# An attention-and-MoE kernel on one core: input queues, the ordering of v in wide products, w2 in 384 columns, and the last weight piece

## The chip, the core and the metric

The kernel runs on one core of one Trainium2 chip. A core has four engines that compute: TensorE (PE in the profile), VectorE (DVE), ScalarE (ACT) and GpSimd (POOL). SyncE (SP) only issues transfers. Products of PE land in PSUM, eight banks of 2 KB in each of 128 partitions; DVE and ACT read them from there into SBUF. Transfers between the chip's memory and SBUF are issued by SP, ACT or POOL, and 16 DMA engines carry them.

The metric is the device time of one execution in microseconds (us), as the median of several runs. Engine times from the profile are microseconds from the start of the span; single durations are in us unless marked ns.

## What is computed

Two layers follow each other. The first is a linear attention with a decaying state, for 4 batches, 8 heads, 768 positions, 48 channels per head:

```
cur  = (u * k_t) outer v_t
y_t  = r_t @ (state + cur)
state = w * state + k_t outer v_t
```

Its output, as x of 3072 rows and 384 columns, goes through a mixture of 8 experts with 4 slots each:

```
logits = x @ phi                       # 3072 x 32
d = softmax over the rows of logits    # which rows a slot takes
c = softmax over the slots             # which slots a row takes back
slot_out[e] = relu((d.T @ x)[e] @ w1[e]) @ w2[e]
out = c @ slot_out
```

w1 and w2 of all experts are 25 MB in float32, r, k and v 14 MB, the output 4.7 MB.

## The kernel before

**Attention.** A pair is two heads of one batch: 4 batches with 4 pairs each, so 16 pairs, numbered m. A pair's 768 positions are halved, and a step i works on one half: pair mu = i // 2, half i % 2. There are 32 steps, with five more ahead of them (i from -5) to fill the pipeline. A half is three blocks of 128 positions. In the code, the blocks are c, the halves g.

Everything is put in program order by hand: the function O keeps each instruction where it was written on its engine, so each engine executes its instructions in the order of the text, and only the waits between engines are added. In step i the order is:

1. a_pe(i+1) and mask_f(i+1): k times r for the next half into the two banks Ab, and DVE's masked copy AT.
2. y_pe(i) and y_evac(i): the result y of this half into columns 0 to 287 of the bank Yb, and ACT's copy of it into x (L372). One bank holds 512 float32 columns.
3. v_pe and v_evac, below.
4. m_pe(i+1) and z_evac(i+1): state and bonus terms into Mb, DVE's products Z (L341) and dv (L342).
5. prod (DVE, even steps), b_pe and kn (odd steps), and scale: POOL multiplies k or r by powers of w (L228) for a later pair.
6. route: what the mixture needs of finished rows: logits and transposes of x into Xb, ACT's copies xT, Le and LexpT; every fourth step also the slot sums (disp, L422 and L426) into columns 768 and up of T0 or T1.
7. t_pe and t_evac: six transposes of kr into T0 (even steps, k) or T1 (odd steps, r), and ACT's copy kT or rT (L241).

**v.** The inputs are loaded with six neighbouring positions of a sequence in one partition (three for v)[...]. v_cast turns a pair's v into bfloat16 (v_bf, L270; the first on POOL), and v_pe puts its rows in order: a product with a shifted selection matrix Q3 for each block c and each j of three, L284. Before the change it does so for one half at a time, two halves ahead: nine products of 96 columns into Vb, and one eviction of 288 columns by ACT (vn, L290).

**Loads.** SP issues w as a single row (L105) and then k, r and v in pieces of two heads. ACT preloads its table and issues w and u once more in another shape (L107, L108). The row w is spread over all partitions by a product (L177), and its logarithm and powers (W, L188 and L192) are needed before the first k can be scaled. POOL issues the weights (L135 for w1, L138 for w2) from step 13 on, in the middle of its scale work, once the last batch's k has landed (guard, L571). w2 takes the buffers of inputs that are used up (raw). The last expert's w2 comes in three pieces of 4, 2 and 2 of its 8 rows y (L576).

**The end.** The first layer of the experts is L623. The second layer (second, L656 to L662) runs four experts side by side in strips of 32 columns of PE; for each row y it takes w2's 384 columns in two products of 192, into Xb and into Yb. DVE and ACT scale a half each into so (L671, L672), and the output is a product of so with LexpT (L684), scaled by DVE and ACT (L686, L688) and written in nine pieces (L704).

Of the kernel before, what the change touches and what calls it, by code (L numbers as in the profile page):

```python
# [9 lines left out]
def kernel(  # L10
# [13 lines left out]
    B, H, S, D = r.shape  # L24
    C = 128
    nC = S // C
    Nn, Dm = out.shape
    ES = moe_phi.shape[1]
    E = moe_w1.shape[0]
    F = moe_w1.shape[2]  # L30
    Spe = ES // E
    nM = Dm // C
    nF = F // C
    nQ = H // 2
    G = 2
    L = nC // G
    T = L * C
    P2 = 2 * D
    nN = Nn // C
    nG = B * G  # L40
    nU = B * nQ
    nH = nU * G
    J = S // C
    JV = T // C

    f32 = mybir.dt.float32
    bf = mybir.dt.bfloat16
    i32 = mybir.dt.int32
    AF = mybir.ActivationFunctionType
    ALU = mybir.AluOpType  # L50

    def O(ins):
        return tc.keep_in_program_order(ins)

    pe, dve, act, pool, sp = nc.tensor, nc.vector, nc.scalar, nc.gpsimd, nc.sync

    big = ctx.enter_context(tc.tile_pool(name="big", bufs=1))
    cst = ctx.enter_context(tc.tile_pool(name="cst", bufs=1))
    wk = ctx.enter_context(tc.tile_pool(name="wk", bufs=3))
# [5 lines left out]
    EG = E // 2  # L65
# [4 lines left out]
    def w2_of(e):  # L70
        g, j = divmod(e, EG)
        return raw[1 + g][:].bitcast(bf)[:, j * eW2:(j + 1) * eW2].rearrange("p (y d) -> p y d", y=nF)

    def raw_of(which, b):
        return raw[b % NR][:, which * RW:(which + 1) * RW]
# [5 lines left out]
    Yb = psb.tile([128, 512], f32, name="Yb")  # L81
    Xb = psb.tile([128, 512], f32, name="Xb")
    Vb = psb.tile([128, 512], f32, name="Vb")
# [11 lines left out]
    w_row = early[0:1, 0:H * D]  # L95
# [5 lines left out]
    phi_f = late[:, 128:128 + nM * ES]  # L101
    wu = cst.tile([8, 128], f32, name="wu")
    wu3 = wu[:].rearrange("q (e s) -> q e s", s=64)
    O(dve.memset(wu[:], 1.0))
    O(sp.dma_start(out=w_row, in_=w.rearrange("(o h) d -> o (h d)", o=1)))  # L105
    O(act.preload_act_table_set("natural_log_exp_and_others"))
    O(act.dma_start(out=wu3[0:4, :, 0:D], in_=w.rearrange("(q e) d -> q e d", e=2)))  # L107
    O(act.dma_start(out=wu3[4:8, :, 0:D], in_=u.rearrange("(q e) d -> q e d", e=2)))  # L108
# [44 lines left out]
    Q3 = cst.tile([128, QW], bf, name="Q3")  # L153
# [59 lines left out]
    ones = cst.tile([128, 128], bf, name="ones")  # L213
    Le_t = [cst.tile([128, L, 128], bf, name=f"Le{j}") for j in range(2)]
    phi_s = cst.tile([128, nM, ES], bf, name="phi_s")
    phi_b = cst.tile([128, nM * ES], bf, name="phi_b")
    assert JV == nM
    acc = cst.tile([128, NA], f32, name="acc")
    guard = cst.tile([128, 1], f32, name="guard")
    st = {}  # L220

# [40 lines left out]
    def v_cast(m):  # L262
        b, q = divmod(m, nQ)
        vb = wk.tile([128, 2, G, JV, D], bf, name="v_bf", bufs=2)
        st["vb", m] = vb
        out, src = vb[:].rearrange("p h g j d -> p (h g j d)"), raw_of(2, b)[:, 2 * q * G * JV * D:2 * (q + 1) * G * JV * D]
        if m == 0:
            O(pool.tensor_copy(out, src))
        else:
            O(act.copy(out, src))  # L270


    def at(i):
        m, g = divmod(i, G)
        b, q = divmod(m, nQ)
        return m, b, q, g, b * G + g

    def v_pe(i):
        m, b, q, g, n = at(i)
        vb = st["vb", m]  # L280
        for c in range(L):
            for j in range(JV):
                o = C * c - j + JV - 1
                O(pe.matmul(Vb[:, c * P2:(c + 1) * P2], Q3[:, o:o + C], vb[:, :, g, j, :],  # L284
                            start=(j == 0), stop=(j == JV - 1)))

    def v_evac(i):
        vn = wk.tile([128, L, 2, D], bf, name="vn", bufs=3)
        st["v", i] = vn
        O(act.copy(vn[:].rearrange("p c e d -> p (c e d)"), Vb[:, 0:L * P2]))  # L290

    def a_pe(i):
        m, b, q, g, n = at(i)
        kT, rT = st["kT", m], st["rT", m]
        for c in range(L):
            t = slice((g * L + c) * C, (g * L + c + 1) * C)
            for e in range(2):
                s = slice(64 * e, 64 * e + 64)
                O(pe.matmul(Ab[:, e, c * C:(c + 1) * C], kT[s, t], rT[s, t]))  # L299
# [129 lines left out]
    def disp_ev(n, ds_p):  # L429
        if n == 0:  # L430
            O(dve.tensor_copy(acc[:], ds_p))
        else:
            O(dve.tensor_add(acc[:], acc[:], ds_p))
# [37 lines left out]
    Wf = [t[:].rearrange("p q j d -> p (q j d)") for t in W]  # L471
# [22 lines left out]
    for i in range(-5, nH):  # L494
        mu, odd = divmod(i, 2)
        if 0 <= i + 1 < nH:
            a_pe(i + 1)
            mask_f(i + 1)
        if pend:
            disp_ev(*pend.pop())  # L500
        if i == nH - 1:
            turn(n0, (2,), Vb[:].bitcast(bf), act)
            disp(n0 - 1, ds_t)
            le_t(n0 - 1)
            let_ev(n0 - 1, None, dve)
        if 0 <= i < nH:
            y_pe(i)
            y_evac(i)
        if 0 <= i + 2 < nH:
            v_pe(i + 2)  # L510
            v_evac(i + 2)
        if 0 <= i + 1 < nH:
            m_pe(i + 1)
            z_evac(i + 1)
        if odd == 0 and 0 <= mu + 1 < nU:
            prod_f(mu + 1)
        if odd and i > 0 and mu + 2 < nU:
            b_pe(mu + 2)
            b_evac(mu + 2)
        if odd and 0 <= mu + 3 < nU:  # L520
            scale(mu + 3, 0)
        if not odd and 0 <= mu + 2 < nU:
            scale(mu + 2, 1)
        route(i, 0)
        if 0 <= mu + 2 < nU:
            t_pe(mu + 2, odd)
            route(i, 1)
            t_evac(mu + 2, odd)
            if odd and i < 0:
                b_pe(mu + 2)  # L530
                b_evac(mu + 2)
        else:
            route(i, 1)
        if odd == 0 and 0 <= mu + 2 < nU:
            v_cast(mu + 2)
        route(i, 2)
        if i == nH - 3:
            turn(n0, (0, 1), T0, act)
        if i == nH - 2:
            turn(n1, (0, 1), T1, act)  # L540
        for f, j, q in T_AT.get(i, ()):
            f(j, q)
        if i in (-4, -3):
            wu_steps(i + 4)
        if i in Z_AT:
            q = Z_AT[i]
            O(act.activation(out=zt[:, q, 2, :], in_=zt[:, q, 0, :], func=AF.Copy, scale=wT[:, q:q + 1]))
        if i == 2:
            O(pool.memset(ones[:], 1.0))
            for t in Le_t:  # L550
                O(pool.memset(t[:], 0.0))
        if i == 3:
            load_kr(0, k, B - 1, 0, H)
            load_kr(1, r, B - 1, 0, H)
            for h0 in range(0, H, 2):
                load_v(B - 1, h0, h0 + 2)
        if i == 5:
            O(act.copy(phi_b[:], phi_f))
        if i == 6:
            for mi in range(nM):  # L560
                for j in range(nM):
                    o = C * mi - j + nM - 1
                    O(pe.matmul(Xb[:, mi * ES:(mi + 1) * ES].rearrange("p (j g s) -> p j g s", g=2, s=Spe),
                                Q3[:, o:o + C],
                                phi_b[:, j * ES:(j + 1) * ES].rearrange("p (g j s) -> p j g s", g=2, s=Spe),
                                start=(j == 0), stop=(j == nM - 1)))
            O(act.copy(phi_s[:].rearrange("p m s -> p (m s)"), Xb[:, 0:nM * ES]))
        if i == 28:
            O(pool.memset(uns, 0.0))
        if i == min(W_AT):  # L570
            O(pool.tensor_copy(guard[:], raw_of(0, B - 1)[:, 0:1]))  # L571
        for _ in range(W_AT.get(i, 0)):
            load_w(nw)
            nw += 1
    assert nw == 2 * E - 1
    for y0, y1 in ((0, 4), (4, 6), (6, 8)):  # L576
        load_w(nw, y0, y1)


# [29 lines left out]
    csr = cst.tile([128, 1], f32, name="csr")  # L609
# [8 lines left out]
    hT = [Wf[1].bitcast(bf)[:, g * F:(g + 1) * F].rearrange("p (y c) -> p y c", c=C) for g in range(2)]  # L618
    for g in range(2):
        for a in range(2):  # L620
            for mi in range(nM):
                for j in range(EG):
                    O(pe.matmul(hb[g][a][32 * j:32 * j + 32, 0:FH], uns[:, mi, g, j, :],  # L623
                                w1_all[:, g * EG + j, mi, a * FH:(a + 1) * FH],
                                start=(mi == 0), stop=(mi == nM - 1), skip_group_check=True))
            src = hb[g][a][:, 0:FH].rearrange("p (q y) -> p y q", y=nF)
            dst = h_sb[g][:, :, a * PH:(a + 1) * PH]
# [12 lines left out]
    def row_recip(a, z):  # L640
        O(dve.reciprocal(rsr[:, a:z], Mb[:, a:z]))

    HD = Dm // 2
# [7 lines left out]
        if g == 0:  # L651
            row_sums(0, 8)
    row_recip(0, 8)
    SO = [Xb[:, 0:HD], Yb[:, 0:HD]]

    def second(g, experts):  # L656
        for y in range(nF):
            for x in range(2):
                for j in experts:
                    O(pe.matmul(SO[x][32 * j:32 * j + 32, :], hT[g][:, y, 32 * j:32 * j + 32],  # L660
                                w2_of(g * EG + j)[:, y, x * HD:(x + 1) * HD],
                                start=(g == 0 and y == 0), stop=(g == 1 and y == nF - 1), skip_group_check=True))  # L662

    second(0, range(EG))
    second(1, range(EG - 2))
# [1 line left out]
    second(1, (EG - 2,))  # L667
    second(1, (EG - 1,))
    row_sums(8, 12)
    so = cst.tile([128, Dm], bf, name="so")  # L670
    O(dve.tensor_scalar_mul(so[:, 0:HD], SO[0], csr[:, 0:1]))  # L671
    O(act.activation(out=so[:, HD:Dm], in_=SO[1], func=AF.Copy, scale=csr[:, 0:1]))  # L672
    row_recip(8, 12)

    out_v = out.rearrange("(p n) m -> p n m", n=nN)
# [14 lines left out]
    i = 0  # L690
# [44 lines left out]
```

The softmax here doesn't subtract the row's maximum and nothing guards it: scores larger than these inputs give would overflow.

## Time and profile before

The median of three runs is 122.65 us (122.47 to 122.68).

| | us |
|---|---|
| profiled execution | 122.36 |
| its span | 120.5 |
| PE busy | 102.6 |
| DVE busy | 96.4 |
| ACT busy | 83.7 |
| POOL busy | 59.7 |
| first input issue of SP (w), then k | 0.74, 1.14 |
| first weight issue of POOL | 40.22 |
| first product of the second layer | 96.36 |
| last weight seen by PE | 103.83 |
| first output issue | 105.56 |

The span is what lies between the first and the last recorded instruction. The rest of the execution, 1.86 us, lies around it. A line of the timeline gives the start, the duration, the engine, the line of the kernel, the operation, output and inputs, the shape, and how many neighbouring instructions are merged; in square brackets stands how long the engine was idle before it and what released it. "PEld" is the loading of weights into PE, "SPq" and "ACTq" the issuing of transfers. The DMA row of the page has a digit for each fortieth of the span, about 3 us: the busy share of the 16 DMA engines in tenths. In the list of waits each line has the waiting engine and line, what it waited for, the sum in us and the number of times. L numbers are lines of the kernel before.

### The profile page before, as it was taken

How to read it: one execution, taken by the hardware profiler on the slowest of the kernel's cores; microseconds unless marked ns; L12 is line 12 of the kernel's file. 1: busy time of each engine (PE TensorE's matmuls, PEld its weight loads, DVE VectorE, ACT ScalarE, POOL GpSimd, SP SyncE). 2: the span in 40 equal slices, each digit the busy share in tenths (PEclk: the TensorE clock that was granted, in tenths of full speed). 3: DMA queues.
4: the chain of work that ended last, by engine and by line, in shares of the span. 5: the costliest groups of instructions: out<-in, count | busy, mean ns of one | idle time of the engine just before them, and what ended most of it. 6: DMA issues, size and time to landing. Idle time of an engine off the chain costs nothing.

```text
span 120.5 us, 4334 instructions
## 1 busy us (share of the span) xinstructions
PE 102.6 (85%) x1795; PEld 82.9 (69%) x1797; DVE 96.4 (80%) x187; ACT 83.7 (69%) x183; POOL 59.7 (50%) x70
## 2 busy tenths in 40 slices
PE   5996977799999999999999999999979996796000
PEld 1465866687887988898888898888866686583000
DVE  6899999999999999899999899999943510399000
ACT  4459769797978998888898988997963510299000
POOL 7349534599999999797677593101000000012000
PEclk9999999999999999999999999999999999999755
DMA  2999999999999999999999999999999998069992
GB/s 38 322 362 373 374 367 371 364 391 362 330 380 382 323 204 216 218 213 212 220 206 222 211 220 209 215 215 215 224 208 220 208 206 165 16 261 389 396 420 100
DMA packets 20925, 31.79 MB, mean 264 GB/s; under 512 B 1129, under 2 KB 18026, under 8 KB 20906
## 3 DMA queue, kind: packets, MB, share of 16 engines
q0 software_dynamic: 2960, 14.55, 55.5%
q1 hardware_dynamic: 17922, 16.96, 41.3%
q8 instruction: 14, 0.23, 0.7%
q14 instruction: 5, 0.04, 0.1%
q10 hardware_dynamic: 24, 0.00, 0.0%
HBM read 39.38 MB, written 4.72 MB: 366 GB/s over the span
## 4 chain that ended last, share of the span: by engine, by line
PE 37%; DMA 31%; DVE 15%; issue 6%; ACT 1%; POOL 1%; POOLq 0%; DVEq 0%; ACTq 0%
DMA raw<-in_moe_w_dram 31%; PE Vb L284 5%; PE T L235 4%; PE Ab L299 4%; PE Yb L352 3%; DVE W L188 3%; PE T L247 2%; PE Mb L325 2%; DVE prod L257 2%; PE Yb L365 2%; DVE kn L252 2%; DVE Z L341 2%; PE Xb L387 2%; PE Xb L380 2%; PE Yb L144 2%
## 5 line engine op out<-in xcount | busy, mean ns | idle before, releaser
L228 POOL TENSOR_TENSOR kr<-raw,W 128x576 bf16<-128x576 f32 x30 | 42.2, 1426 | 12.4 <-PE T L235 5.2
L304 DVE TENSOR_TENSOR AT<-Ab,mask_ut 128x768 bf16<-128x768 f32 x32 | 30.2, 945 | 0.8 <-PE Ab L299 0.6
L284 PE MATMUL Vb<-v_bf,Q 128*128 128x96 bf16 x288 | 18.2, 211 | 0.0
L235 PE MATMUL T<-ident,kr 128*128 128x128 bf16 x192 | 17.2, 230 | 1.0 <-POOL kr L228 1.0
L284 PEld LDWEIGHTS <-Q 128*128 128x128 bf16 x288 | 16.3, 100 | 1.5 <-issue 0.2
L241 ACT COPY kT<-T 128x768 bf16<-128x768 bf16 x16 | 12.8, 799 | 4.6 <-PE T L235 3.3
L241 ACT COPY rT<-T 128x768 bf16<-128x768 bf16 x16 | 12.8, 800 | 4.2 <-PE T L235 3.6
L257 DVE TENSOR_TENSOR prod<-T,kT 128x768 bf16<-128x768 bf16 x16 | 15.2, 947 | 0.0
L342 DVE TENSOR_TENSOR dv<-vn,Mb 128x288 bf16<-128x288 bf16 x32 | 14.1, 440 | 0.0
L235 PEld LDWEIGHTS <-kr 128*128 128x128 bf16 x192 | 12.7, 102 | 1.8 <-POOL kr L228 1.2
L290 ACT CAST vn<-Vb 128x288 bf16<-128x288 f32 x32 | 13.4, 419 | 0.1
L372 ACT CAST x<-Yb 128x288 bf16<-128x288 f32 x32 | 13.1, 409 | 0.2 <-PE Yb L365 0.2
L341 DVE TENSOR_TENSOR Z<-Mb,zt 128x288 bf16<-128x288 f32 (+1 forms) x32 | 12.7, 395 | 0.6
L299 PE MATMUL Ab<-rT,kT 64*128 64x128 bf16 x192 | 11.1, 222 | 2.1 <-DVE AT L304 2.1
L704 POOL DMA_DIRECT2D out_dram<-W x1 | 0.5, 549 | 24.9 <-DVE W L686 24.9
L325 PE MATMUL Mb<-vn,kn 128*128 128x96 bf16 (+2 forms) x80 | 11.5, 242 | 0.0
L352 PE MATMUL Yb<-vn,AT 128*128 128x48 bf16 x192 | 10.3, 185 | 0.1
L270 ACT CAST v_bf<-raw 128x576 bf16<-128x576 f32 x15 | 10.2, 677 | 0.0
L299 PEld LDWEIGHTS <-kT 64*128 64x128 bf16 x192 | 5.6, 95 | 5.6 <-DVE AT L304 2.0
L138 POOL DMA_DIRECT2D raw<-in_moe_w_dram x10 | 5.5, 557 | 7.9 <-DMA raw<-in_moe_w_dram 6.5
L352 PEld LDWEIGHTS <-AT 128*128 128x128 bf16 x192 | 7.1, 96 | 3.3
L365 PE MATMUL Yb<-dv,ident 128*128 128x288 bf16 x32 | 9.1, 285 | 0.2
(143 smaller groups left out, 221.7 us busy)
## 6 DMA issues: line engine op xcount, KB each, us to landing
w_all<-in_moe_w_dram POOLq DMA_DIRECT2D x8, 768.0 KB, 12.7
raw<-in_moe_w_dram POOLq DMA_DIRECT2D x7, 768.0 KB, 18.4
raw<-in_v_dram SPq DMA_DIRECT2D x12, 288.0 KB, 6.2
raw<-in_k_dram SPq DMA_DIRECT2D x8, 288.0 KB, 6.1
raw<-in_r_dram SPq DMA_DIRECT2D x8, 288.0 KB, 5.9
raw<-in_k_dram SPq DMA_DIRECT2D x2, 1152.0 KB, 12.9
raw<-in_r_dram SPq DMA_DIRECT2D x2, 1152.0 KB, 10.3
out_dram<-raw POOLq DMA_DIRECT2D x2, 768.0 KB, 6.8
```

Source lines behind the costliest of these rows:

```text
L228: O(eng.tensor_mul(kr[:, j].rearrange("p j (h s) -> p j h s", s=64)[:, :, :, 0:D], src, W[j][:, q].rearrange("p j (h d) -> p j h d", h=2)))
L235: O(pe.transpose(bank[:, x * C:(x + 1) * C], kr[:, j, x, :], ident[:]))
L241: O(act.copy(t[:].rearrange("p (s j) -> p s j", j=J), bank[:, 0:S].rearrange("p (j s) -> p s j", j=J)))
L257: O(dve.tensor_mul(pr[:].rearrange("p (s j) -> p s j", j=J), T1[:, 0:S].rearrange("p (j s) -> p s j", j=J), st["kT", m][:].rearrange("p (s ...
L284: O(pe.matmul(Vb[:, c * P2:(c + 1) * P2], Q3[:, o:o + C], vb[:, :, g, j, :], start=(j == 0), stop=(j == JV - 1)))
L290: O(act.copy(vn[:].rearrange("p c e d -> p (c e d)"), Vb[:, 0:L * P2]))
L299: O(pe.matmul(Ab[:, e, c * C:(c + 1) * C], kT[s, t], rT[s, t]))
L304: O(dve.tensor_mul(AT[:], Ab[:, :, 0:T].rearrange("p e (c t) -> p e c t", c=L), mask_ut[:, None, None, :].to_broadcast([128, 2, L, C])))
L325: O(pe.matmul(o, kn[:, g * L + c, :], vc, start=first, stop=True, skip_group_check=True))
L341: O(dve.tensor_mul(Z[:], Mb[:, 0:x * P2].rearrange("p (c e) -> p c e", c=x), zt[:, q, 0:x, :]))
L342: O(dve.tensor_mul(dv[:], st["v", i][:].rearrange("p c e d -> p (c e) d"), Mb[:, 288:288 + 2 * L, None].to_broadcast([128, L * 2, D])))
L352: O(pe.matmul(Yb[:, o:o + D], AT[:, e, c, :], vn[:, c, e, :], start=first, stop=False, skip_group_check=True))
```

## The change

- w's row is issued by ACT ahead of its table load; k is then the first load on SP's queue.
- v_pe works on a whole pair: nine products of 192 columns, both halves side by side. Blocks 0 and 1 go to Vb (384 columns), block 2 to columns 320 to 511 of Yb. v_evac copies them in two parts, 384 columns from Vb and 192 from Yb, into vn, which holds a pair and has two buffers in place of three for halves. Both run in even steps, one pair ahead.
- v_cast moves from the even step, after kT's eviction, to the odd step, ahead of m_pe and so ahead of rT's eviction.
- The tile phi_b now lies in the memory of acc, and the tile `so` in a part of W that is not used any more at that point.
- The second layer takes w2's 384 columns in one product, into Xb alone; DVE and ACT scale a half each of that bank.
- The last expert's w2 comes in pieces of 4, 3 and 1 rows.

```diff
-    O(sp.dma_start(out=w_row, in_=w.rearrange("(o h) d -> o (h d)", o=1)))
+    O(act.dma_start(out=w_row, in_=w.rearrange("(o h) d -> o (h d)", o=1)))
...
+    phi_b = acc[:].bitcast(bf)[:, 0:nM * ES]
...
-    def v_pe(i):
-        m, b, q, g, n = at(i)
+    VW = G * P2
+
+    def v_pe(m):
         vb = st["vb", m]
         for c in range(L):
+            dst = Vb[:, c * VW:(c + 1) * VW] if c < 2 else Yb[:, 512 - VW:512]
             for j in range(JV):
                 o = C * c - j + JV - 1
-                O(pe.matmul(Vb[:, c * P2:(c + 1) * P2], Q3[:, o:o + C], vb[:, :, g, j, :],
-                            start=(j == 0), stop=(j == JV - 1)))
+                O(pe.matmul(dst.rearrange("p (g e d) -> p g e d", g=G, e=2), Q3[:, o:o + C],
+                            vb[:, :, :, j, :].rearrange("p e g d -> p g e d"),
+                            start=(j == 0), stop=(j == JV - 1), skip_group_check=True))
...
-        vn = wk.tile([128, L, 2, D], bf, name="vn", bufs=3)
-        st["v", i] = vn
-        O(act.copy(vn[:].rearrange("p c e d -> p (c e d)"), Vb[:, 0:L * P2]))
+        vn = wk.tile([128, G, L, 2, D], bf, name="vn", bufs=2)
+        for g in range(G):
+            st["v", m * G + g] = vn[:, g]
+        O(act.copy(vn[:, :, 0:2].rearrange("p g c e d -> p g c (e d)"),
+                   Vb[:, 0:2 * VW].rearrange("p (c g x) -> p g c x", c=2, g=G)))
+        O(act.copy(vn[:, :, 2].rearrange("p g e d -> p g (e d)"),
+                   Yb[:, 512 - VW:512].rearrange("p (g x) -> p g x", g=G)))
...
             y_pe(i)
             y_evac(i)
-        if 0 <= i + 2 < nH:
-            v_pe(i + 2)
-            v_evac(i + 2)
+        if i == -4 or (odd and 1 <= mu + 2 < nU):
+            v_cast(mu + 2)
+        if odd == 0 and 0 <= mu + 1 < nU:
+            v_pe(mu + 1)
+            v_evac(mu + 1)
...
-        if odd == 0 and 0 <= mu + 2 < nU:
-            v_cast(mu + 2)
...
-    for y0, y1 in ((0, 4), (4, 6), (6, 8)):
+    for y0, y1 in ((0, 4), (4, 7), (7, 8)):
...
-    SO = [Xb[:, 0:HD], Yb[:, 0:HD]]
+    SO = Xb[:, 0:Dm]
...
-            for x in range(2):
-                for j in experts:
-                    O(pe.matmul(SO[x][32 * j:32 * j + 32, :], hT[g][:, y, 32 * j:32 * j + 32],
-                                w2_of(g * EG + j)[:, y, x * HD:(x + 1) * HD],
+            for j in experts:
+                O(pe.matmul(SO[32 * j:32 * j + 32, :], hT[g][:, y, 32 * j:32 * j + 32],
+                            w2_of(g * EG + j)[:, y, :],
...
-    so = cst.tile([128, Dm], bf, name="so")
-    O(dve.tensor_scalar_mul(so[:, 0:HD], SO[0], csr[:, 0:1]))
-    O(act.activation(out=so[:, HD:Dm], in_=SO[1], func=AF.Copy, scale=csr[:, 0:1]))
+    so = Wf[1].bitcast(bf)[:, 2 * F + nM * ES * 8:2 * F + nM * ES * 8 + Dm]
+    O(dve.tensor_scalar_mul(so[:, 0:HD], SO[:, 0:HD], csr[:, 0:1]))
+    O(act.activation(out=so[:, HD:Dm], in_=SO[:, HD:Dm], func=AF.Copy, scale=csr[:, 0:1]))
```

More of the change, by code (lines that the diff above doesn't have):

```diff
@@ L215 @@
     phi_s = cst.tile([128, nM, ES], bf, name="phi_s")
-    phi_b = cst.tile([128, nM * ES], bf, name="phi_b")
     assert JV == nM
     acc = cst.tile([128, NA], f32, name="acc")
+    phi_b = acc[:].bitcast(bf)[:, 0:nM * ES]
     guard = cst.tile([128, 1], f32, name="guard")
@@ L276, in at, with v_evac @@
         return m, b, q, g, b * G + g
-    def v_pe(i):
-        m, b, q, g, n = at(i)
+    VW = G * P2
+    def v_pe(m):
         vb = st["vb", m]
         for c in range(L):
+            dst = Vb[:, c * VW:(c + 1) * VW] if c < 2 else Yb[:, 512 - VW:512]
             for j in range(JV):
                 o = C * c - j + JV - 1
-                O(pe.matmul(Vb[:, c * P2:(c + 1) * P2], Q3[:, o:o + C], vb[:, :, g, j, :],
-                            start=(j == 0), stop=(j == JV - 1)))
-    def v_evac(i):
-        vn = wk.tile([128, L, 2, D], bf, name="vn", bufs=3)
-        st["v", i] = vn
-        O(act.copy(vn[:].rearrange("p c e d -> p (c e d)"), Vb[:, 0:L * P2]))
+                O(pe.matmul(dst.rearrange("p (g e d) -> p g e d", g=G, e=2), Q3[:, o:o + C],
+                            vb[:, :, :, j, :].rearrange("p e g d -> p g e d"),
+                            start=(j == 0), stop=(j == JV - 1), skip_group_check=True))
+    def v_evac(m):
+        vn = wk.tile([128, G, L, 2, D], bf, name="vn", bufs=2)
[5 more added lines that the diff above has]
+                   Yb[:, 512 - VW:512].rearrange("p (g x) -> p g x", g=G)))
     def a_pe(i):
@@ L557 @@
         if i == 5:
-            O(act.copy(phi_b[:], phi_f))
+            O(act.copy(phi_b, phi_f))
         if i == 6:
@@ L653 @@
     row_recip(0, 8)
-    SO = [Xb[:, 0:HD], Yb[:, 0:HD]]
+    SO = Xb[:, 0:Dm]
     def second(g, experts):
         for y in range(nF):
-            for x in range(2):
-                for j in experts:
-                    O(pe.matmul(SO[x][32 * j:32 * j + 32, :], hT[g][:, y, 32 * j:32 * j + 32],
-                                w2_of(g * EG + j)[:, y, x * HD:(x + 1) * HD],
-                                start=(g == 0 and y == 0), stop=(g == 1 and y == nF - 1), skip_group_check=True))
+            for j in experts:
+                O(pe.matmul(SO[32 * j:32 * j + 32, :], hT[g][:, y, 32 * j:32 * j + 32],
+                            w2_of(g * EG + j)[:, y, :],
+                            start=(g == 0 and y == 0), stop=(g == 1 and y == nF - 1), skip_group_check=True))
     second(0, range(EG))
```

## The prediction

> **What bounds the kernel now.** I read the page first (busy shares, slices, the chain that ended last), then the stretch around the last weights, then the pair loop, then the start.
>
> ```profile
> PE 102.6 (85%) x1795; PEld 82.9 (69%) x1797; DVE 96.4 (80%) x187; ACT 83.7 (69%) x183; POOL 59.7 (50%) x70
> ...
> DMA  2999999999999999999999999999999998069992
> ...
> PE 37%; DMA 31%; DVE 15%; issue 6%; ACT 1%; POOL 1%; POOLq 0%; DVEq 0%; ACTq 0%
> ```
>
> The DMA row is full from slice 1 to slice 32: inputs first, then 16 experts' weights. The chain ends on a weight. At the end PE sits waiting for the last piece of w2:
>
> ```profile
> 98.93 0.25 PE L660 MATMUL Yb<-raw,W 128*32 128x192 bf16 x2
> ...
> 103.83 0.24 PE L660 MATMUL Xb<-raw,W 128*32 128x192 bf16 x1 [0.41 <-DMA raw<-in_moe_w_dram]
> ...
> 104.28 0.42 DVE L671 TENSOR_SCALAR so<-Xb,csr 128x192 bf16<-128x192 f32 x1 [7.27 <-PE Xb L660]
> ...
> 104.36 0.42 ACT L672 ACTIVATE so<-Yb,csr 128x192 bf16<-128x192 f32 x1 [7.53 <-PE Yb L660]
> ```
>
> So the end is weight-bound, but not by far. The second layer starts on PE at 96.36; with all weights there it needs 96.36 to 99.02 (six experts), some 0.16 filler, then 2 x 16 products at 0.083 spacing (1.33 each), that is to 101.86. It issues its last at 104.16. **Compute has 2.3 us of slack**, no more. After it the output stream runs at full DMA from 106.5 to 118.2, so a later first output is a later end by as much.
>
> The pair loop (two steps to a pair, four pairs from kT at 60.03 to 79.06, 4.76 each) is PE-bound with DVE just behind. Two views of it matter:
>
> ```profile
> ACT kT L241 <- PE T L426: 1.1, 2, 0.5
> ...
> PEld L380 <- ACT xT L396: 1.4, 7, 0.2
> ...
> ACT rT L241 <- PE T L426: 0.7, 2, 0.3
> ```
>
> ```profile
> 58.00 0.80 ACT L241 COPY rT<-T 128x768 bf16<-128x768 bf16 x1 [0.24 <-PE T L235]
> ...
> 58.42 0.28 PE L365 MATMUL Yb<-dv,ident 128*128 128x288 bf16 x1
> ...
> 58.54 0.55 PE L284 MATMUL Vb<-v_bf,Q 128*128 128x96 bf16 x9
> ...
> 58.70 0.49 ACT L396 COPY xT<-Xb 128x384 bf16<-128x384 bf16 x1
> ...
> 59.07 0.42 ACT L372 CAST x<-Yb 128x288 bf16<-128x288 f32 x1
> ```
>
> In the waits the evictions of kT and rT (columns 0 to 767 of T0, T1) are released by L426, a product into columns 768 and up of the same bank: waits are kept by bank, not by column. In the timeline of an even step, PE ends y (L365) and starts v (L284) at 58.54, while ACT is still with rT and xT and reads y out of Yb only from 59.07 to 59.49. PE does not care today, as v goes to Vb.
>
> **What the skill says.** "PSUM — Partial Sum Buffer", section "PSUM bank collisions raise a hardware error": two engines on one bank and quadrant collide even at different columns, reads against reads too, and the compiler's scheduler orders such pairs. The L426 releases agree for PE against ACT; no run here shows read against read. "DMA: Bandwidth & Descriptors", section "Queues, rings and completion order": a DMA engine alternates between queues packet by packet; no row here shows SP and ACT loads competing. Price: "ScalarE: Activation LUTs", "What ACT_TABLE_LOAD costs": 186 ns + 0.833 N, some 93 ns overlapped. For 288 columns 426 ns; the row has 419.
>
> **The change part by part.**
>
> *k first, w on ACT.* w's issue (0.74 to 1.08) leaves SP, k goes from 1.14 to 0.74, every input 0.40 us earlier. w's one packet ran at 1.71 and landed at 2.09, its reader L177 starts at 3.13 behind four warming products: about 1 us of cover, against an ACT issue of 0.65 (its later load of u) in place of 0.34. The table load and the wu, u loads behind it on ACT's queue move by at most 0.65; the first ACTIVATE is at 3.91 (table load of 1.28 done by about 2.7), wu's reader at 7.70. Cost 0. If DMA stays the bound: -0.40.
>
> *Wide v.* 18 products of 96 columns a pair (0.34 to 0.38 a step, twice) become 9 of 192. At 0.083 each, 0.75: nothing either way (-0.05 to +0.05 a pair). The evictions change from two of 288 (0.42) to one of 384 and one of 192: estimate from the price 0.51 and 0.35, less overlap the same ACT time. The tiles phi_b (now in acc) and `so` (now in W) lie in buffers that are idle then: 0.
>
> *The third block goes to Yb, and this is the part that decides.* In an even step PE issues y, then blocks 0 and 1 into Vb (6 x 0.08 = 0.48), then block 2 into Yb. By the bank rule block 2 waits until ACT has read y out. Behind it in PE's queue stand m, the x transposes, kr's transposes, the next A and y, so DVE's Z, prod and AT wait too. The stall is (end of x's eviction, minus start of v, + 0.05 for the release, taken from xT 61.78 to L380 61.83) - 0.48. The rows give end minus start for each even step. Moving v_cast doesn't shorten it: rT waits for its transposes (0.24 idle above) and xT and x follow it on ACT.
> - Loop, steps 10 to 28: 0.95, 1.09, 0.95, 0.76, 0.95, 1.09, 0.94, 0.76, 0.95, 1.08 us. Less 0.43 each: 9.52 - 4.30 = 5.2.
> - Steps 4, 6, 8: 0.60, 0.59, 0.60. There DVE is the bound: Z could follow AT at once (26.39 + 0.86 = 27.25); m now ends 0.38 + 0.17 later, 27.36, + 0.11 = 27.47. 0.22 each: 0.7.
> - Steps 0 and 2, where x stands on ACT behind an exponential that waits for DVE:
>
> ```profile
> 15.33 0.55 PE L284 MATMUL Vb<-v_bf,Q 128*128 128x96 bf16 x9
> ...
> 16.23 0.68 ACT L192 ACTIVATE W<-W 128x576 f32<-128x576 f32 x1 [0.98 <-DVE W L188]
> ...
> 16.99 0.34 DVE L341 TENSOR_TENSOR Z<-Mb,zt 128x192 bf16<-128x192 f32 x1
> ...
> 17.09 0.38 ACT L372 CAST x<-Yb 128x288 bf16<-128x288 f32 x1
> ```
>
> x ends at 17.47, block 2 runs 17.52 to 17.76, m to 18.1, Z at 18.2 instead of 16.99: DVE, busy without a gap here, loses 1.2. Step 2 repeats it (v 20.99, x ends 23.31, Z was at 22.84): 1.25. Together 2.5.
>
> *v_cast into the odd step, ahead of rT.* It fills ACT's wait for rT's transposes and leaves the even step, where it made xT late: PE's waits for xT (1.4 in all) should go. -1.4. rT itself comes no later (x 0.29 + cast 0.58 ends at about 1.06 after y, transposes end at 1.38). If this cover were gone, rT would be up to 0.3 late a pair.
>
> Delay of compute: 2.5 + 0.7 + 5.2 - 1.4 = 7.0 us.
>
> *w2 in 384 columns, last piece one row.* 64 products at 0.16 for 128 at 0.083: nothing. The bytes are the same, packets take 0.248 us for 3072 B and 0.135 for 1536 B, linear, so the last piece still lands at 103.84 less what the stream gains; one product for four after it: -0.1 if weight-bound. But SO now lies in one bank: if ACT must wait for DVE's read of it, its half of `so` begins 0.42 later instead of 0.08: +0.34 (0 if they may overlap, 0.4 with a release). I take 0.34.
>
> *Side effect on the weights.* POOL issues the first weight at 40.22 behind kr products that need buffers freed by transposes (step 8). With compute 3 us late there it issues about 2.2 late; the input stream ends on most engines at 41 to 42, so they idle: weights end 0.6 to 1.8 later. Below the compute delay, thus hidden.
>
> **Sum.** Profiled execution 122.36 (span 120.5 and 1.86 around it). 7.0 - 2.3 slack + 0.34 = +5.0: 127.4. The median is 0.29 above this execution; I forecast 127.5.
>
> **Bounds of the unknown costs.** Start 1.2 (only one of the two stalls stays) to 2.6; steps 4 to 8, 0 to 0.8; loop net 2.0 (ACT catches up earlier once PE is slower) to 4.5; `so` 0 to 0.4. Compute delay 3.2 to 7.9, end 123.6 to 128.7.
>
> **Rivals.**
> - *Forecast, 0.62*: Yb's wait, compute takes over as the bound, 127.5. For: both orders are written in the code, and every term has a row. Against: the sum adds eleven stalls as if nothing recovered.
> - *The wait is there but most is absorbed, 0.16*: PE and DVE both have small gaps, compute delay near 2.5; then the late weights decide: 122.65 + about 1.3 + 0.34 = 124.3.
> - *No wait, 0.22*: block 2 lies in columns 320 to 511, y in 0 to 287. If the order is kept by column, the loop is as fast as before and only the weight stream counts: -0.40 - 0.1 + 0.34 = 122.5, or 122.15 if the halves of `so` overlap. It decides as soon as the compute delay is below 1.9 (2.3 less the 0.4 that the stream gains). For: today nothing in the trace shows a PE write held by an ACT read of other columns. Against: L426.
>
> A measurement of this kernel can tell 0.2% (0.25 us) from no change. Slower 0.62 + 0.15; faster 0.15 out of the last case; same 0.08 out of the last two. Likeliest case alone 123.6 to 128.7; to leave no more than 2 in 10 out, 122.4 to 128.7.
>
> **What would show it.** Right: a wait of a Yb product of v on ACT's x (L372), near 0.5 us each and over 1 us in steps 0 and 2; second layer near 103 without waits for weights between its experts; first weight issue after 42. k's first issue near 0.74. L672 starting when L671 ends. Wrong: last weight landing still the releaser of the last w2 product, the pair near 4.7, PE with no gap after L372.

## The result, and the profile after

| | before | after |
|---|---|---|
| median of six runs, us | 122.52 (122.4 to 122.68) | 129.97 (129.59 to 130.4) |
| profiled execution, its span | 122.36, 120.5 | 129.78, 128.0 |
| first product of the second layer | 96.36 | 106.16 |
| first output issue | 105.56 | 113.02 |

The ratio is 1.061, 95% interval 1.0583 to 1.0637: slower by 7.4 us, where 5.0 were forecast and 128.7 was the upper end of the range. (L numbers of the kernel after are six or seven higher than before from v on: x is L379, Z L348, prod L257, the bonus product into Mb L336, `so` L677 and L678.)

The page of the kernel after: busy shares, the DMA row by slices, and the chain that ended last, by engine and by line.

```profile
PE 103.2 (81%) x1587; PEld 79.8 (62%) x1589; DVE 97.2 (76%) x187; ACT 85.4 (67%) x183; POOL 59.2 (46%) x70
...
DMA  3999999999999699999999999999999940049992
...
PE 40%; DVE 28%; ACT 16%; issue 9%; POOLq 0%; DVEq 0%; ACTq 0%
DVE prod L257 11%; ACT rT L241 6%; DVE dv L349 5%; PE Yb L286 5%; PE T L247 4%; PE T L235 4%; PE Xb L666 4%; PE Mb L336 3%; DVE W L188 3%; ACT x L379 3%; ACT xT L403 2%; DVE AT L311 2%; PE Mb L332 2%; PE Yb L144 1%; DVE kn L252 1%
```

DMA, 31% of the chain before, is gone from it. The busy times of PE, DVE and ACT rose by no more than 1.7 us, so the 7.5 us that the span gained are waiting, not work. The chain runs through prod, rT, dv, v's third block (Yb L286) and x in turn. The list of waits of the kernel after (waiting engine and line, what for, us in total, times, longest) names the same partners:

```profile
DVE Z L348 <- PE Mb L336: 9.7, 15, 1.2
...
PEld L336 <- DVE prod L257: 5.4, 13, 1.3
PE Yb L286 <- ACT x L379: 5.4, 10, 1.7
...
PE Mb L336 <- DVE prod L257: 2.4, 6, 1.1
```

None of these four is in the list before, and the wait of PE's weight loads for xT that stood there (1.4) is gone. The start shows the forecast wait as it was drawn. Timeline of the kernel after, step 0:

```profile
16.45 0.68 ACT L192 ACTIVATE W<-W 128x576 f32<-128x576 f32 x1 [1.17 <-DVE W L188]
...
17.30 0.38 ACT L379 CAST x<-Yb 128x288 bf16<-128x288 f32 x1
17.73 0.41 PE L286 MATMUL Yb<-v_bf,Q 128*128 128x192 bf16 x3 [0.58 <-ACT x L379]
...
18.44 0.36 DVE L348 TENSOR_TENSOR Z<-Mb,zt 128x192 bf16<-128x192 f32 x1 [1.16 <-PE Mb L336]
```

ACT's copy x of columns 0 to 287 ends at 17.68, and the product into columns 320 to 511 starts at 17.73. All 15 third blocks of the trace from step 0 on start about 0.05 after such a copy ends. So the order is kept by bank and not by column, as the Trainium skill asks of a kernel ("PSUM — Partial Sum Buffer", section "PSUM bank collisions raise a hardware error"). Yb is one tile that fills one bank, so no run tells an order by bank from an order by tile.

The best single measure of the delay is the start of Z, one per step, after minus before: 1.45 at step 1, 2.68 at step 3, 3.54 at step 9, 9.81 at step 29 and at step 31. (Z of an odd step i is made in the even step i - 1, where the wait stands.) So the start costs 2.7, steps 4 to 8 0.86, and the loop, from step 9 to step 29, 6.27.

Now the loop, a pair from Z at 66.17 to Z at 71.40. Timeline of the kernel after:

```profile
66.17 0.36 DVE L348 TENSOR_TENSOR Z<-Mb,zt 128x192 bf16<-128x192 f32 x1 [0.58 <-PE Mb L336]
...
66.81 0.95 DVE L257 TENSOR_TENSOR prod<-T,kT 128x768 bf16<-128x768 bf16 x1
...
67.81 0.14 PEld L336 LDWEIGHTS <-prod 128*128 128x128 bf16 x3 [0.23 <-DVE prod L257]
67.82 0.23 PE L336 MATMUL Mb<-ucol,prod 128*128 128x2 bf16 x3
...
68.48 0.50 PE L235 MATMUL T<-ident,kr 128*128 128x128 bf16 x6
...
69.02 0.80 ACT L241 COPY rT<-T 128x768 bf16<-128x768 bf16 x1 [0.19 <-PE T L235]
...
69.85 0.49 ACT L403 COPY xT<-Xb 128x384 bf16<-128x384 bf16 x1
70.21 0.43 ACT L379 CAST x<-Yb 128x288 bf16<-128x288 f32 x1
...
70.69 0.41 PE L286 MATMUL Yb<-v_bf,Q 128*128 128x192 bf16 x3 [0.48 <-ACT x L379]
...
71.40 0.36 DVE L348 TENSOR_TENSOR Z<-Mb,zt 128x192 bf16<-128x192 f32 x1 [0.72 <-PE Mb L336]
```

Read it as a ring. A late v block makes Mb late, and so Z. Behind Z on DVE stand dv and prod; PE's bonus product of the odd step needs prod (67.76) and idles until 67.81. Behind that product on PE stand the transposes that rT needs; behind rT on ACT stand xT and x; and x releases the next v block. The starts give the ring's length: Z and dv 0.64 (66.17 to 66.81), prod and its release 1.00 (to 67.81), from the load of prod to the transposes 0.67 (to 68.48), transposes 0.54 (to 69.02), rT and xT 1.19 (to 70.21), x 0.48 (to 70.69), block and Mb 0.71 (to 71.40): 5.23. In the kernel before, the same pair takes 4.60:

```profile
59.40 0.34 DVE L341 TENSOR_TENSOR Z<-Mb,zt 128x192 bf16<-128x192 f32 x1
...
64.00 0.36 DVE L341 TENSOR_TENSOR Z<-Mb,zt 128x192 bf16<-128x192 f32 x1
```

The chain agrees: prod has 11% of 128.0 us, 14 us, which is all but one of the 16 prods at 0.95.

Busy time between the same two Z (steps 9 and 29), kernel before and then after; the columns are the length, and PE, PEld, DVE, ACT and POOL busy:

```profile
36.09:83.04 46.95, 46.62 (x940) 39.89 (x937) 45.69 (x85) 41.53 (x94) 33.03 (x36) 1.00 1.05 232
```

```profile
39.63:92.85 53.22, 47.73 (x858) 39.72 (x856) 45.91 (x84) 43.32 (x96) 30.89 (x35) 1.00 1.01 211
```

Ten pairs took 46.95 and take 53.22. Before, PE had 0.3 us of idle time and DVE 1.3. After, PE has 5.5 and DVE 7.3: no single engine is the bound, the waits from one engine to the next are.

The end of the kernel after, where the two halves of `so` are read:

```profile
111.37 0.42 DVE L677 TENSOR_SCALAR W<-Xb,csr 128x192 bf16<-128x192 f32 x1 [4.56 <-PE Xb L666]
...
111.82 0.42 ACT L678 ACTIVATE W<-Xb,csr 128x192 bf16<-128x192 f32 x1 [5.19 <-DVE W L677]
```

ACT's half of `so` starts 0.45 after DVE's half of the same bank, against 0.08 before. All products of the second layer run without a wait for a weight.

### The profile page after: what moved, and what is told of

Its sections match the earlier page's. It is cut to its first block, busy times and chain, and to the rows that moved or that the text cites. A ratio compares the mean times of both kernels' runs of the same rounds, so it can differ in the third digit from the quotient of the medians.

```text
span 128.0 us, 3900 instructions
## 1 busy us (share of the span) xinstructions
PE 103.2 (81%) x1587; PEld 79.8 (62%) x1589; DVE 97.2 (76%) x187; ACT 85.4 (67%) x183; POOL 59.2 (46%) x70
## 4 chain that ended last, share of the span: by engine, by line
PE 40%; DVE 28%; ACT 16%; issue 9%; POOLq 0%; DVEq 0%; ACTq 0%
DVE prod L257 11%; ACT rT L241 6%; DVE dv L349 5%; PE Yb L286 5%; PE T L247 4%; PE T L235 4%; PE Xb L666 4%; PE Mb L336 3%; DVE W L188 3%; ACT x L379 3%; ACT xT L403 2%; DVE AT L311 2%; PE Mb L332 2%; PE Yb L144 1%; DVE kn L252 1%
## 5 line engine op out<-in xcount | busy, mean ns | idle before, releaser
L348 DVE TENSOR_TENSOR Z<-Mb,zt 128x288 bf16<-128x288 f32 (+1 forms) x32 | 12.8, 401 | 9.7 <-PE Mb L336 9.7
L286 PEld LDWEIGHTS <-Q 128*128 128x128 bf16 x144 | 13.3, 102 | 9.0 <-issue 7.5
L257 DVE TENSOR_TENSOR prod<-T,kT 128x768 bf16<-128x768 bf16 x16 | 15.2, 950 | 0.0
L379 ACT CAST x<-Yb 128x288 bf16<-128x288 f32 x32 | 13.1, 410 | 0.4
L286 PE MATMUL Vb<-v_bf,Q 128*128 128x192 bf16 x96 | 11.4, 259 | 0.0
L286 PE MATMUL Yb<-v_bf,Q 128*128 128x192 bf16 x48 | 6.5, 244 | 5.7 <-ACT x L379 5.4
L336 PE MATMUL Mb<-ucol,prod 128*128 128x2 bf16 x96 | 7.1, 166 | 3.0 <-DVE prod L257 2.4
L247 PE MATMUL T<-ident,kT 128*128 128x128 bf16 x96 | 8.6, 230 | 1.1 <-DVE acc L440 0.5
```

What stands on the lines that cost most here:

```text
L247: O(pe.transpose(T0[:, c * C:(c + 1) * C], kT[:, c * C:(c + 1) * C], ident[:]))
L257: O(dve.tensor_mul(pr[:].rearrange("p (s j) -> p s j", j=J), T1[:, 0:S].rearrange("p (j s) -> p s j", j=J), st["kT", m][:].rearrange("p (s ...
L286: O(pe.matmul(dst.rearrange("p (g e d) -> p g e d", g=G, e=2), Q3[:, o:o + C], vb[:, :, :, j, :].rearrange("p e g d -> p g e d"), start=(j ...
L348: O(dve.tensor_mul(Z[:], Mb[:, 0:x * P2].rearrange("p (c e) -> p c e", c=x), zt[:, q, 0:x, :]))
L379: O(act.copy(st["x", n][:, :, q * P2:(q + 1) * P2], Yb[:, 0:L * P2].rearrange("p (c e) -> p c e", c=L)))
```

## The experiments

Delays are starts of Z against the kernel before, in one profiled execution each. Times are medians, each with its ratio to runs of the kernel before on the same chip (medians 122.66 to 122.69).

### All of the change but v (e1), and v alone (e2)

e1 is the kernel after with v_pe, v_evac, their call and v_cast as before:

```diff
-        if i == -4 or (odd and 1 <= mu + 2 < nU):
-            v_cast(mu + 2)
-        if odd == 0 and 0 <= mu + 1 < nU:
-            v_pe(mu + 1)
-            v_evac(mu + 1)
+        if 0 <= i + 2 < nH:
+            v_pe(i + 2)
+            v_evac(i + 2)
...
+        if odd == 0 and 0 <= mu + 2 < nU:
+            v_cast(mu + 2)
```

e2 is the kernel before with the reverse of this edit, and with the places of phi_b and `so` of the change, to make room.

> The changed kernel with v put back: products and evictions half by half into Vb, v_cast in the even step; the input queues, w2 in 384 columns and the last piece stay. Both theories (bank wait; wide v as such) put the whole loss into v, so the loop returns to 4.7 to 4.8 us a pair and the end is weight-bound: k first -0.4, last piece -0.1, the two reads of one bank +0.37 (L678 waited for L677 in the changed kernel): 122.4, within 0.3. Over 124 would mean that another part of the change costs.

> The kernel before with the v part alone (wide products, block 2 in Yb, v_cast in the odd step, the two tiles moved to make room). Both theories: compute is the bound, so k first and the last piece are worth nothing there, and only the 0.37 us of the second read goes: 129.6. Delay of Z by step as in the changed kernel: 2.7 at step 3, 9.8 at step 31.

e1: 122.85, ratio 1.0026 (1.0003 to 1.0049). Its Z delay is 0.5 from step 1 on and stays there, and its chain is again that of a weight-bound end:

```profile
PE 39%; DMA 34%; DVE 8%; issue 5%; POOL 4%; ACT 2%; POOLq 0%; DVEq 0%; ACTq 0%
```

e2: 130.61, ratio 1.0657 (1.06 to 1.0714); Z delay 2.47 at step 3 and 10.38 at step 31. The whole loss belongs to v. All the rest together costs 0.2 against the runs beside it; the 122.4 expected had counted on 0.4 from k first, which e5 below does not find. e2 came 1.0 above its expectation. Its loop is as long as that of the kernel after (Z delay 4.10 at step 9, 10.39 at step 29). Steps 4 to 8 cost 1.6 in place of 0.86, in a stretch where its trace shows a lower granted clock (6 tenths in the ninth slice) and that of the kernel after does not; the rest of the 1.0 stays open.

### Block 2 later (e3), prod earlier (e4)

e3 leaves the wide products as they are and moves only the third block and its copy to a place where x has long been read:

```diff
-            v_pe(mu + 1)
-            v_evac(mu + 1)
+            v_pe(mu + 1, (0, 1))
+            v_evac(mu + 1, False)
...
         route(i, 0)
+        if odd == 0 and 0 <= mu + 1 < nU:
+            v_pe(mu + 1, (2,))
+            v_evac(mu + 1, True)
```

e4 leaves the wait where it is and takes prod out from behind Z on DVE:

```diff
+        if odd == 0 and 0 <= mu + 1 < nU:
+            prod_f(mu + 1)
         if 0 <= i + 1 < nH:
             m_pe(i + 1)
             z_evac(i + 1)
-        if odd == 0 and 0 <= mu + 1 < nU:
-            prod_f(mu + 1)
```

> The changed kernel with block 2 of v and its eviction moved down PE's and ACT's order, behind m, the logits and the transposes of x, and ahead of kr's transposes. Same products, same bank. Bank-wait theory: ACT has read y by then (v start + 0.48 + 0.34 + 0.26 = 1.08 against 0.95 to 1.09 for the end of its read), the wait shrinks to under 0.1 in the loop and in steps 0 and 2 no longer holds Z; compute delay at step 31 under 3, end weight-bound, 122.4 to 123.2. Rival (wide v as such: uneven steps, two evictions): stays over 127.

> The changed kernel with DVE's prod moved ahead of m and Z in the even step, so that DVE works on prod while Z waits for block 2. Theory of the ring (Z late, prod late behind it, the next step's bonus product L336 waits for prod, so rT, xT, x and the next block 2 come late): L336's waits (5.4 us in the list of waits) go, the loop's share of the delay falls from 6.3 to 3.8 or less, 127.4 or under. Rival (the prediction missed no such dependence, and ACT's longer evictions account for the rest): L336's waits fall but the time stays at 129.5 to 130.3.

e3: 122.55, ratio 0.9994 (0.9968 to 1.0019). Z delay 0.0 at steps 1 and 3, 0.17 at step 9, -0.29 at step 31. These readings are from an execution of 125.33, well above the median, whose extra time lies behind the loop: in the second layer PE waits 2.97 for a weight, and the granted clock is lower there. Of the wait for x two at the start are left, harmless there:

```profile
PE Yb L286 <- ACT x L382: 2.8, 2, 1.4
```

So 7.4 us hang on the place of three products and one copy in the order. That v is ordered in wide products costs nothing that shows in the time; of compute it may cost some, since v_cast's move alone gains 1.0 in the loop (f1 below) and e3, which has that move too, gains no more than 0.5 there.

e4: 125.64, ratio 1.0218 (1.0166 to 1.0271). Its list of waits:

```profile
PE Yb L286 <- ACT x L379: 6.6, 11, 1.7
...
DVE AT L311 <- PE Ab L306: 2.9, 9, 0.6
```

The wait for x is all there, even a little longer. Of L336's waits for prod one is left (1.3), ahead of the loop. In this kernel prod comes ahead of Z in the even steps, which makes the Z that is made there, that of an odd step, up to 0.9 later than its neighbours, so odd steps are compared with odd ones and even with even. From step 9 to step 29 the Z delay grows from 2.72 to 6.16, by 3.4. From step 10 to step 30, whose Z has no prod ahead of it, it grows from 1.85 to 5.69, by 3.8:

```profile
40.30 0.44 DVE L348 TENSOR_TENSOR Z<-Mb,zt 128x288 bf16<-128x288 f32 x1
...
91.26 0.45 DVE L348 TENSOR_TENSOR Z<-Mb,zt 128x288 bf16<-128x288 f32 x1
```

In the kernel after, both differences are 6.3. So the wait stays, and about three fifths of the loop's loss stay with it; the other two fifths, 2.4 to 2.8 us, go once the link from prod to L336 is taken out of the ring. (e4's move of prod was not run in the kernel before, whose list has no wait for prod.)

### The cast's move alone (f1), and taken back (f2)

The sum credits v_cast's move with 1.4. f1 makes that move in the kernel before; f2 takes it back in the kernel after. The edit of f1 (f2 is its reverse):

```diff
+        if i == -4 or (odd and 1 <= mu + 2 < nU):
+            v_cast(mu + 2)
         if 0 <= i + 2 < nH:
             v_pe(i + 2)
...
-        if odd == 0 and 0 <= mu + 2 < nU:
-            v_cast(mu + 2)
```

> The kernel before, with v_cast alone moved from the even step (behind kT's eviction) to the odd step (ahead of the v products and rT's eviction). The sum on record credits this with -1.4 of compute delay, taken from PE's waits for xT. If that holds: those waits gone, Z of the last step 0.8 to 1.4 earlier than before, second layer near 95.2, the time within 0.3 of before (122.3 to 122.9) as the end is bound by the weights. Rival: the waits for xT were not on the path; Z of the last step within 0.3 of before.

> The changed kernel with v_cast alone put back into the even step, behind kT's eviction and ahead of xT. Ring theory: cast (0.69) pushes xT's copy from 67.47 to 68.07, PE's L387 from 68.18 to about 68.6, and rT, x and the third v block behind it by the same 0.42, once a pair, as PE, ACT and DVE wait for each other in turn: some ten pairs, +4 on the changed kernel: 133 to 135, Z of the last step 13 to 14.5 later than before. Rival, the credit as the sum has it: +1.4, 131.0 to 131.8. Second rival: the moved cast does nothing, 129.6 to 130.4.

f1: 122.88, ratio 1.0011 (0.9995 to 1.0026). Z delay 0.21 at step 1 and -0.79 at step 31: 1.0 gained in the pair loop, hidden at the end by the weights, as expected, and the waits for xT are gone from its list. f2: 132.12, ratio 1.0754 (1.071 to 1.0798), that is 2.15 above the kernel after; Z delay 12.42 at step 31. The ring theory had +4 and the plain credit +1.4, so neither size was met. The wait that comes back in f2 goes with a smaller cost than +4: it occurs six times in ten pairs, with 0.35 at most, 1.9 in all.

```profile
PEld L387 <- ACT xT L403: 1.9, 6, 0.3
```

The credit of 1.4 was thus sound in kind, and larger in the kernel after than the sum had it. With it taken back, the loop alone (steps 9 to 29, 4.10 to 12.42) costs 8.3, which is 2.0 more than in the kernel after.

### The small parts: k first (e5), last piece (e6), w2 in one bank (e7)

Each is one of the change's edits alone in the kernel before: w's load on ACT; pieces of 4, 3 and 1 rows; SO in Xb alone with products of 384 columns.

```diff
-    O(sp.dma_start(out=w_row, in_=w.rearrange("(o h) d -> o (h d)", o=1)))
+    O(act.dma_start(out=w_row, in_=w.rearrange("(o h) d -> o (h d)", o=1)))
```

```diff
-    for y0, y1 in ((0, 4), (4, 6), (6, 8)):
+    for y0, y1 in ((0, 4), (4, 7), (7, 8)):
```

```diff
-    SO = [Xb[:, 0:HD], Yb[:, 0:HD]]
+    SO = Xb[:, 0:Dm]
```

> The kernel before with one line changed: w's row issued by ACT ahead of its table load, k first on SP. If the input stream moves as a whole and the weights follow it (the prediction), the last weight lands 0.40 earlier: 122.25 against 122.65. Rival: the first weight is issued when POOL's scale work allows (40.2), which doesn't move, so the DMA engines that finish the inputs early wait and the end stays within 0.15 of before.

> The kernel before with pieces of 4, 3 and 1 rows of the last w2. One or two products fewer after the last landing: -0.1. Rival: the pieces of 3 rows lands later than that of 2 and its products stand in the way, no change within 0.1.

> The kernel before with w2 in 384 columns into one bank. If ACT's read of the bank waits for DVE's, as L678 did for L677 in the changed kernel, the first output is issued 0.37 later and the time is 122.65 + 0.35 = 123.0. If something else held L678 there: 122.65 within 0.1.

e5: 122.72, ratio 1.0005 (0.9983 to 1.0026): nothing, not -0.40. k's issue does move from 1.14 to 0.73, but batch 3's k is issued at 24.42 against 24.41, and the last input lands at 43.2 in both. SP's own list of waits in e5, from 17 to 40 us, shows what batch 3's loads wait for:

```profile
SPq L115 <- POOL kr L228: 6.6, 2, 5.0
```

In the kernel before it is 6.4. POOL's kr products read the buffers that batch 3's k and r are to fill, so these loads go when compute lets them, however early the first one went. POOL's first weight issue came at 40.40 against 40.22: the rival in the expectation came true. w itself costs nothing on ACT: its reader L177 starts at 3.13 as before.

e6: 122.56, ratio 0.9989 (0.9973 to 1.0005): the expected -0.1, not told from nothing.

e7: 123.09, ratio 1.0038 (1.0025 to 1.0051), +0.4. The timeline of e7 shows where:

```profile
104.43 0.42 DVE L670 TENSOR_SCALAR so<-Xb,csr 128x192 bf16<-128x192 f32 x1 [7.43 <-PE Xb L659]
104.88 0.42 ACT L671 ACTIVATE so<-Xb,csr 128x192 bf16<-128x192 f32 x1 [8.06 <-DVE so L670]
```

### The parts that cost taken out (e8)

The kernel after with e3's late block and with w2's halves in two banks again.

> Block 2 of v moved down as in the earlier run, and w2 back in two products and two banks; wide v, v_cast's place, k first and the last piece stay. Bank-wait theory: Z of step 31 at most where it was before the change, no wait of a Yb product of over 0.2 us in the loop, end weight-bound. From the parts: -0.4 (k first) - 0.1 (last piece) = 122.2; if k first is worth nothing, 122.6.

123.2, ratio 1.0021 (1.0 to 1.0042): the loss is gone, and nothing is gained. Its Z delay is 1.82 by step 4 and 1.57 at step 31, below the slack, and its end is weight-bound. The expectation that Z of step 31 would be no later than before was not met. In its profiled execution TensorE's granted clock was lower in slices 5 to 9 than in that of the kernel before (digits 7 7 9 8 5, against 9 in the page of the kernel before, whose clock record begins only at 24.9 us), the stretch in which the delay arose. By e7 it should have been 0.4 shorter than e3, from which it differs in w2's halves alone, and it came out 0.65 longer; that stays open. No version tried beats the kernel before by more than the measurement can tell.

## Why the prediction came out as it did

- **The wait of block 2 for x**: right in kind, place and cause. Start 2.5 forecast, 2.7 measured (2.47 in e2, 2.49 in f2, where the first step lost 0.2 less; the fifth slice of the kernel after shows 6 tenths of the clock, theirs 9). Steps 4 to 8 0.7 forecast, 0.86 measured, and 1.6 in e2 and f2 with the lower clock there.
- **The step that failed is the loop's: "0.95, 1.09, 0.95, 0.76, ... us. Less 0.43 each: 9.52 - 4.30 = 5.2."** It took the place of x's end from the rows of before and priced each stall on PE alone. But prod stands behind the delayed Z on DVE, PE's odd step waits for prod, and so rT and x come late too. The prediction names prod among what waits; the way back from prod to x it had at nothing. Without the cast's move this loop cost 8.3 (f2) for 5.2; with it, 6.27 for 3.8. With prod out of the way it cost 3.4 to 3.8 (e4), which is what the sum had for a loop in which only PE waits. That the two agree so closely is in part luck: the list of waits for x in e4's loop comes to 3.3, not to 5.2. The trace of the kernel after, between steps 9 and 29, lists 3.1 of waits for x and 2.4 of L336's loads for prod. PE's idle time grew there by 5.2 and its busy time by 1.1, together the 6.27; what the 1.1 is was not resolved.
- **v_cast, -1.4**: right in kind: 1.0 in f1; in the kernel after 2.0 of delay in the loop and 2.15 of time (f2). It isn't the cause of the miss.
- **Slack 2.3**: Z was 9.8 late and the second layer 9.8, `so` on DVE 7.1 (111.37 against 104.28): 2.7 were absorbed.
- **Second read of one bank, +0.34**: 0.45 against 0.08 before, so +0.37; e7 alone +0.4 in time. The Trainium skill ("PSUM — Partial Sum Buffer", section "PSUM bank collisions raise a hardware error") counts reads against reads; the prediction said no run showed it, and now the kernel after and e7 do.
- **k first, -0.40 if the weights decide**: it had no part in the forecast, as compute hides it, but it stood in the rivals; e5 shows that it is nothing where the weights do decide.
- **Late weights, hidden**: right, with a size a little off. The first weight issue came at 41.75 (forecast: past 42) against 40.22, and no product of the second layer waited for one.

Sum by measurement: 9.81 - 2.7 + 0.37 = 7.5, against 7.46 at the first output. Of the 2.4 us that the forecast missed, the loop makes 2.5, the start and steps 4 to 8 0.4, and the larger slack takes 0.4 back. (The forecast's own terms add up to 122.36 + 5.0 + 0.29 = 127.7, where it says 127.5; nothing turns on it.)

The signs that the prediction named for "right" are there in kind: the waits for x, a second layer without waits for weights, k's issue at 0.74, and ACT's half of `so` starting as DVE's ends. Three sizes differ. The waits are 0.34 to 0.5 in the loop and 1.71 in step 2, but 0.58 in step 0 (1.62 in e2, where the clock was not low ahead of it). The second layer starts at 106.16, not near 103. The first weight issue lies 0.25 before the bound it gave.

## What to carry to other kernels

Where two engines are both nearly full (here 46.62 and 45.69 of 46.95), a stall on one is not a sum over its own rows: follow what stands behind the delayed instruction on each engine in turn, and if the path comes back to the stall's own releaser, price the length of the ring and not the stall. A free range of columns is no free place as long as another engine has yet to read the same bank; put the write after that read in program order, where the loss was gone (e3). And test an earlier load at the end of its stream, not at its start: here 0.4 us of lead was gone at the first loads that wait for buffers.

## What the runs showed of the hardware that was not expected

- Two reads of one PSUM bank by DVE and ACT, at different columns, ran one after the other: 0.45 from start to start for 128x192 float32 with a duration of 0.42 each (kernel after and e7); in two banks, in the kernel before, 0.08.
- Kernels with the same early work differed at step 1 by a constant offset: 0.2 us in e5, e6 and f1, whose fifth slice shows a granted clock of 5 or 6 tenths, and none in e7, with 9. e1 has 0.5 with a 9 there, but the clock record in its trace begins only at 17.5 us, so that 9 was not measured. Its six transposes at 14.23 took 0.85 in place of 0.52, as long as those of the kernel after at 14.24, where the clock is on record at 0.50; so a low clock is likely in e1 too, and not shown. Compare differences of delays between steps, then, not the delays.
